# Last fourth-product rows at the end, fewer matmuls in the second half, sums by accumulating DMAs: one change to an FFT-convolution and MLP kernel

## The chip, the cores and the metric

The kernel runs on one core of one Trainium2 chip. The metric is the device time of one execution in microseconds (us); three runs of a kernel give its median. The engines are PE (matrix products into PSUM), ACT (activations, and nearly all copies out of PSUM), DVE (elementwise work), POOL (small work, and the issue of some DMAs) and SP (the issue of most DMAs).

## What is computed

The reference, cut to what matters (2048 rows, 640 columns, bf16 throughout):

```
x = A_q;  g = sigmoid((x * gate_w).sum(-1))
# a: long convolution
kv = (short 4-tap convolution of k along the rows) * v
y  = irfft(rfft(kv padded to 4096) * rfft(ssm_k padded to 4096))[:2048] + kv * ssm_D
a  = x * y
# b: two small MLPs
h  = gelu(layernorm(x) @ w1)                 # 640 -> 640
x1 = x + (h, four column groups shifted by 1, -1, 2, -2 rows) @ w2
b  = x1 + gelu(layernorm(x1) @ w3) @ w4      # 640 -> 1536 -> 640
out = g * a + (1 - g) * b
```

## The kernel before, in words

Everything lives in one SBUF tensor, `arena`. Row `1024 c + 8 p + rho` of an input lies on partition p, so the 2048 rows are 16 tiles (c = 0, 1; rho = 0 to 7) of 128 x 640. `X` holds x, later x1, later b, and in the end the output.

**The MLP side.** `ln1_rows` normalizes a pair of tiles on DVE (tag xn), transposes it on PE in ten pieces (xTp) and copies the result with one ACT operation of 1280 elements (xTe). Then come the first product (mm1, `gelu1`), the second (mm2, evicted to x1, with sums of squares on ACT), the second layernorm with transposes by DMA (xT, issued by SP), the third product (mm3: ten matmuls of 512 columns, `gelu3`) and the fourth (mm4: 24 matmuls of 320 columns for one tile). mm3 and mm4 run over four groups of rows, `sc` = 0 to 3, with six mm3 jobs and four mm4 jobs each. A job is a set of matmuls into one of four pairs of PSUM banks, with its evictions.

**The convolution side.** DVE makes kv from k and v (tags kv, kvb) in four blocks. The long convolution is a real transform of length 4096, split by hand: matmuls with cosine tables make parts of the transform (`forward`, fwdh for ssm_k and fwdk for kv), and DVE does the rest of it elementwise. It works on two halves of 320 columns (half 0, 1) and on two sets of 128 frequencies (kap = 0, 1). `unit(half, kap, ...)` is DVE's part: a `butterfly` of each signal (bh, bk), a `window` of kv, the complex product (`pointwise`, pw, pwz) and a `fold`. It is written in operations of 2560 and 1280 elements per partition. In each unit one addition of 2560 elements is done by a DMA that adds into its destination (`add_dma`, tag pwa, issued by POOL). For even r the transform of set 1 is got from the PSUM sums of set 0 with one more weight (`FM2`, two matmuls); for odd r it takes four matmuls of its own (`FM1`). `inverse(half, ...)` makes eight products, one for each rho, of eight matmuls each, evicts them with the gate g as scale (gy), multiplies them by q on DVE (fin), adds them to X, and stores. In half 0 that last sum is an accumulating DMA (fina); in half 1 it is DVE's, and the last four products are split into pieces of 320 (invl, gyl, finl).

**The order.** Nothing runs by loops at run time. The program collects nodes (one instruction or one matmul job each) with their dependences, and `schedule` puts them in one order with the help of a list of ranks and a forward model; each engine then executes its nodes in that order, waiting on semaphores. SP's and POOL's DMAs are nodes of their queues and stand in order as well: a waiting one holds those behind it.

The names and lines that the prediction uses: L663 is DVE's `tensor_tensor`, L694 every eviction by ACT, L1147 mm4, L1129 mm3, L1178 the transforms (`forward`), L1366 and L1341 the inverse products, L927 the transposes of the first layernorm, L702 `add_dma`, L868 a small POOL operation of the layernorms, L706 loads, L912 and L906 small layernorm operations on DVE.

Of the kernel before, what the change touches and what calls it, by code (L numbers as in the profile page):

```python
# [7 lines left out]
U16 = mybir.dt.uint16  # L8
# [4 lines left out]
PAIRS = 4  # L13
# [75 lines left out]
class Prog:  # L89
    LAT = {"pe": (0.0, 0.20), "act": (0.24, 0.16), "dve": (0.12, 0.12), "pool": (0.2, 0.2), "sp": (0.1, 0.1)}  # L90
    LOOK = 1.0

# [86 lines left out]
    PRIO = ()  # L179

    def schedule(self):
        for n in self.nodes:
            n.base = frozenset(n.deps)
        for j in self.jobs:
            own = set(j.nodes)
            j.ext = [d for v in j.nodes if not v.first for d in v.base if d not in own]
            if j.seeded:
                j.nodes[0].soft = [d for v in j.pes for d in v.base if d not in own]
        for n in self.nodes:
            for d in n.deps:  # L190
                d.users.append(n)
        for n in self.nodes:
            n.prio = self.PRIO[n.idx]
        self._forward()

    RATE = 390e3
    WINDOW = 3.4133
    PHASE = 2.4

    def _forward(self):  # L200
        nodes = self.nodes
        for n in nodes:
            n.deps = set(n.base)
            n.missing = len(n.deps)
            n.start = n.end = None
        for j in self.jobs:
            j.pair = None
            j.left = len(j.evicts) if j.evicts else 1
        free = {"pe": 1.0, "act": 0.7, "dve": 0.8, "pool": 1.1, "sp": 0.7}
        ready = {e: [] for e in ENGS}  # L210
        known_at = {}
        pair_free = [0.0] * PAIRS
        pair_job = [None] * PAIRS
        bits = [[False, False] for _ in range(PAIRS)]
        link = 0.0
        xlink = 0.0
        alink = 0.0
        slink = 0.0
        warm = False
        window = -1  # L220
        duty = carry = 0.0
        busy, lock = False, 0.0
        LAT = self.LAT

        def arrive(n):
            at = 0.0
            for d in n.deps:
                t = d.end + (LAT[d.eng][0 if d.eng == n.eng else 1] if d.kind == "c" else 0.05)
                if t > at:
                    at = t  # L230
            known_at[n] = at
            ready[n.eng].append(n)

        for n in nodes:
            if n.missing == 0:
                arrive(n)
        left = len(nodes)
        order = {e: [] for e in ENGS}
        allseq = []
        while left:  # L240
            best = None
            for e in ENGS:
                for n in ready[e]:
                    t = max(known_at[n], free[e])
                    if n.first:
                        j = n.job
                        tp = None
                        for i in range(PAIRS):
                            if pair_job[i] is not None and pair_job[i].left:
                                continue  # L250
                            if j.seeded and not (bits[i][0] and bits[i][1]):
                                continue
                            if tp is None or pair_free[i] < tp:
                                tp = pair_free[i]
                        if tp is None:
                            continue
                        t = max(t, tp)
                        ok = True
                        for d in j.ext:
                            if d.end is None:  # L260
                                ok = False
                                break
                            if not n.seed:
                                t = max(t, d.end - n.cost)
                        if ok and n.seed:
                            for d in n.soft:
                                if d.end is None:
                                    ok = False
                                    break
                                t = max(t, d.end - self.LOOK)  # L270
                        if not ok:
                            continue
                    key = (t, -n.prio, n.idx)
                    if best is None or key < best[0]:
                        best = (key, n)
            assert best is not None, "schedule is stuck"
            n = best[1]
            e = n.eng
            t = best[0][0]
            ready[e].remove(n)  # L280
            n.start = t
            cost = n.cost
            if n.array:
                w = int((t - self.PHASE) // self.WINDOW)
                while window < w:
                    warm = duty > (0.42 if warm else 0.75) * self.WINDOW
                    window += 1
                    duty, carry = carry, 0.0
                if not warm:
                    cost += n.array  # L290
                if n.tag != "shk":
                    inside = min(cost, self.PHASE + (w + 1) * self.WINDOW - t)
                    duty += inside
                    carry += cost - inside
            if n.kind == "c" and e == "pool":
                if busy and free["dve"] > t + 0.2:
                    cost *= 2.2
                lock = t + cost
            elif e == "dve":
                busy = n.cost > 0.3 and n.tag[:2] != "bn"  # L300
                if busy and lock > t + 0.1:
                    cost += 0.48
                    lock = 0.0
            free[e] = t + cost
            if n.kind == "xpose":
                free[e] = max(free[e], link - 1.5)
            if n.kind == "c":
                n.end = t + cost
            elif n.kind == "dma":
                link = max(link, xlink, t + 1.2) + n.bytes / self.RATE  # L310
                n.end = link + n.land
            elif n.kind == "acc":
                alink = link = max(alink, link, t + 1.2) + n.bytes / 220e3
                n.end = alink + 1.6
            elif n.kind == "side":
                slink = max(slink, t + 1.0) + 0.2
                n.end = slink + (6.5 if link > t else 2.8)
            else:
                xlink = max(xlink, t + 1.3, link) + n.bytes / 190e3
                n.end = xlink + 0.5  # L320
            j = n.job
            if n.first:
                pick = None
                for i in range(PAIRS):
                    if pair_job[i] is not None and pair_job[i].left:
                        continue
                    if j.seeded and not (bits[i][0] and bits[i][1]):
                        continue
                    if pick is None or pair_free[i] < pair_free[pick]:
                        pick = i  # L330
                j.pair = pick
                if pair_job[pick] is not None:
                    old = pair_job[pick]
                    n.deps.update(old.evicts if old.evicts else old.pes)
                pair_job[pick] = j
                for b in range(2):
                    if j.bits[b] is not None:
                        bits[pick][b] = j.bits[b]
            if j is not None and (n in j.evicts or not j.evicts):
                j.left -= 1  # L340
                if j.left == 0:
                    ends = [v.end for v in (j.evicts or j.pes)]
                    pair_free[j.pair] = max(ends) + 0.1
            n.seq = len(allseq)
            n.ordinal = len(order[e])
            order[e].append(n)
            allseq.append(n)
            left -= 1
            for u in n.users:
                u.missing -= 1  # L350
                if u.missing == 0:
                    arrive(u)
        self.order = order
        self.allseq = allseq
        self.span = max(n.end for n in nodes if n.tag[:4] != "fill")
        while order["pe"][-1].tag[:4] == "fill":
            order["pe"].pop()
# [37 lines left out]
    def emit(self, block):  # L395
# [11 lines left out]
        for n in self.nodes:  # L407
            if n.kind != "c":
                n.sem = nc.alloc_semaphore(f"d{n.idx}")
# [104 lines left out]

def _tables():

# [929 lines left out]
```

## Time and profile before

| what | value |
|---|---|
| three runs | 225.59, 225.94, 227.07 us, median 225.94 |
| profiled execution, first to last instruction | 223.5 us (of this execution no other time is listed; the median of the runs is 2.4 us longer than its span) |
| PE, DVE, ACT, POOL busy | 97%, 93%, 78%, 18% of the span |
| granted TensorE clock, mean | 0.998 |
| DMA traffic | 34.04 MB, mean 152 GB/s |

How to read it: "busy" is the union of an engine's instructions, so PE at 97% has hardly a gap. Rows of a view by form read: line, engine, operation, output and input shape, count, then busy time in us and mean time of one in ns, then the engine's idle time just ahead of them with who ended it. DMA rows give the count, the size and the median us from issue to landing.

### The profile page before, as it was taken

Reading aid. Unit: us, or ns where it says so; the run is one execution under the profiler, and the core shown is the slowest. Engines: PE = TensorE matmul, PEld = TensorE weight load, DVE = VectorE, ACT = ScalarE, POOL = GpSimd, SP = SyncE. Lnnn points to the kernel's source line nnn. Section 1 sums busy time; section 2 is a strip of 40 time slices with the busy share of each in tenths; the row PEclk is TensorE's granted clock in tenths of the full one; section 3 lists DMA queues with packets and bytes.
Section 4 is the critical chain, followed back from the end, with each engine's and each line's share of the span. In section 5 each row is a group of like instructions: output and inputs, shape, how many; then the busy total and the mean of one; then the engine's idle time right before and its main releaser. Section 6 shows DMA issues by size and latency. Waiting matters only on the chain.

```text
span 223.5 us, 3945 instructions
## 1 busy us (share of the span) xinstructions
PE 216.3 (97%) x1557; PEld 138.0 (62%) x1569; DVE 208.7 (93%) x267; ACT 174.6 (78%) x292; POOL 41.1 (18%) x48
## 2 busy tenths in 40 slices
PE   7999999999999999999999999999999999999993
PEld 7589655557676655457744455667745675577772
DVE  4999899999999899999899999799998999999976
ACT  3989999899999999999987488997145723572484
POOL 1335662403003120450200200000020002033020
PEclk9999999999999999999999999999999999999999
DMA  6999996589801968061654150003559000648667
GB/s 208 385 403 387 350 361 236 116 156 283 349 5 33 345 120 337 4 117 41 126 101 90 24 97 0 1 3 98 137 87 257 11 0 3 117 87 117 151 117 235
DMA packets 36713, 34.04 MB, mean 152 GB/s; under 512 B 17508, under 2 KB 31719, under 8 KB 36568
## 3 DMA queue, kind: packets, MB, share of 16 engines
q1 hardware_dynamic: 31560, 23.97, 35.8%
q0 software_dynamic: 4848, 9.50, 18.9%
q10 hardware_dynamic: 288, 0.33, 0.6%
q8 instruction: 12, 0.20, 0.4%
q14 instruction: 5, 0.04, 0.1%
HBM read 21.47 MB, written 3.93 MB: 114 GB/s over the span
## 4 chain that ended last, share of the span: by engine, by line
PE 76%; ACT 18%; DVE 2%; DMA 2%; issue 1%; SPq 0%; ACTq 0%
PE PS L1147 23%; PE PS L1129 23%; ACT arena L694 12%; PE PS L1178 9%; PE PS L967 8%; PE PS L1366 6%; ACT PS L1057 5%; PE PS L927 2%; ACT arena L680 2%; DVE arena L663 2%; DMA arena<-in_A_q_dram 2%; PE PS L823 1%; PE PS L769 1%; PE PS L758 1%; PE PS L780 0%
## 5 line engine op out<-in xcount | busy, mean ns | idle before, releaser
L663 DVE TENSOR_TENSOR arena<-arena 128x2560 bf16<-128x2560 bf16 (+5 forms) x175 | 186.1, 1116 | 7.0 <-ACT arena L694 3.5
L694 ACT ACTIVATE arena<-PS 128x640 bf16<-128x640 f32 (+8 forms) x142 | 104.2, 812 | 18.9 <-PE PS L1129 14.7
L1147 PE MATMUL PS<-arena 128*128 128x320 bf16 x384 | 53.3, 299 | 0.0
L1129 PE MATMUL PS<-arena 128*128 128x512 bf16 x232 | 52.2, 379 | 0.8 <-ACT arena L694 0.5
L1147 PEld LDWEIGHTS PS<-arena 128*128 128x128 bf16 x384 | 37.4, 98 | 15.0 <-issue 0.3
L694 ACT ACTIVATE arena<-PS,arena 128x320 bf16<-128x320 f32 (+1 forms) x47 | 27.7, 626 | 24.2 <-PE PS L1147 22.2
L1129 PEld LDWEIGHTS PS<-arena 128*128 128x128 bf16 x240 | 23.3, 98 | 27.4 <-issue 0.5
L1178 PE MATMUL PS<-arena 128*128 128x320 bf16 x224 | 34.4, 300 | 0.7 <-DVE arena L906 0.6
L1178 PEld LDWEIGHTS PS<-arena 128*128 128x128 bf16 x224 | 20.8, 98 | 12.8 <-ACT arena L694 2.8
L680 ACT ACTIVATE arena<-arena 128x640 bf16<-128x640 bf16 (+2 forms) x34 | 25.8, 787 | 0.8 <-DMA arena<-in_A_q_dram 0.4
L967 PE MATMUL PS<-arena 128*128 128x512 bf16 (+1 forms) x121 | 22.9, 335 | 0.2
L1075 PE MATMUL PS<-arena 128*128 128x320 bf16 x160 | 22.6, 299 | 0.0
L1057 ACT ACTIVATE PS<-arena 128x640 f32<-128x640 bf16 x32 | 22.3, 719 | 0.2
L868 POOL TENSOR_TENSOR arena<-arena 128x4 f32<-128x4 f32 (+1 forms) x9 | 14.0, 1553 | 30.7 <-DVE arena L668 30.4
L1075 PEld LDWEIGHTS PS<-arena 128*128 128x128 bf16 x160 | 15.4, 98 | 6.7 <-ACT PS L1057 0.6
L967 PEld LDWEIGHTS PS<-arena 128*128 128x128 bf16 x125 | 11.8, 98 | 8.2 <-ACT arena L694 0.5
L702 POOL DMA_DIRECT2D arena<-arena x4 | 4.8, 1202 | 57.6 <-DVE arena L663 57.6
L888 DVE BATCH_NORM_STATS2 arena<-arena 128x6 f32<-128x320 bf16 x28 | 12.4, 477 | 2.9 <-DMA arena<-in_A_q_dram 2.8
L1366 PE MATMUL PS<-arena 128*128 128x320 bf16 x96 | 14.3, 299 | 0.0
L1007 POOL DMA_DIRECT2D arena<-arena x18 | 9.7, 545 | 12.7 <-ACT arena L694 12.7
L1366 PEld LDWEIGHTS PS<-arena 128*128 128x128 bf16 x96 | 9.2, 98 | 4.3 <-issue 0.3
L1392 POOL DMA_DIRECT2D arena<-arena x4 | 5.1, 1276 | 35.7 <-ACT arena L694 25.9
(42 smaller groups left out, 81.5 us busy)
## 6 DMA issues: line engine op xcount, KB each, us to landing
arena<-in_B_w_dram POOLq DMA_DIRECT2D x4, 960.0 KB, 8.2
arena<-in_A_k_dram SPq DMA_DIRECT2D x4, 640.0 KB, 14.3
arena<-in_A_v_dram SPq DMA_DIRECT2D x4, 640.0 KB, 14.1
arena<-arena POOLq DMA_DIRECT2D x4, 640.0 KB, 6.1
arena<-in_A_q_dram SPq DMA_DIRECT2D x4, 640.0 KB, 7.4
out_dram<-arena SPq DMA_DIRECT2D x15, 160.0 KB, 2.0
arena<-in_A_q_dram SPq DMA_DIRECT2D x6, 320.0 KB, 5.5
arena<-in_A_ssm_k_dram SPq DMA_DIRECT2D x3, 512.0 KB, 11.5
```

The lines of the kernel that those rows point to most:

```text
L663: return dve(lambda e: e.tensor_tensor(o, a, b, op), [a, b], [o], c_tt(n), tag=tag, **kw)
L680: node = P.op("act", lambda e, ps: e.activation(o, i, func, **kw), r=r, w=[o], cost=c_act(n, naps, acc is not None, psum=False), tag=tag, ...
L694: node = P.op("act", lambda e, ps: e.activation(ov, inner(ps), func, **kw), r=r, w=[o], cost=c_act(n, len(r), acc is not None), job=job, t ...
L868: P.op("pool", lambda e, ps: e.tensor_tensor(r, v, hv, ALU.pow), r=[v, HALF], w=[r], cost=cost, tag="ln")
L888: dve(lambda e, o=o, x=x: e.bn_stats(o, x), [x], [o], 0.393, tag="bn", group=("bn", id(mv), rho, c))
L967: fns.append(lambda e, ps, b=b, c=c, lhsT=lhsT: e.matmul(bank(ps, b, 256 * n), lhsT, XT[:, c, r0:r0 + n, :], start=(c == 0), stop=(c == 4)))
L1057: P.seed(job, lambda e, ps: e.activation(two(ps, 320), x, ACTF.Copy), [X[:, c, rho, :]], c_act(640, psum=False), tag)
L1075: fns.append(lambda e, ps, hh=hh, ft=ft, lhsT=lhsT: e.matmul(bank(ps, hh, 320), lhsT, w2v[:, ft, 320 * hh:320 * hh + 320], start=False, st ...
L1129: fns.append(lambda e, ps, b=b, ft=ft, c=c, sc=sc: e.matmul(bank(ps, b, 512), w3h[ft // 6][:, c, 128 * (ft % 6):128 * (ft % 6) + 128], XT[ ...
L1147: fns.append(lambda e, ps, hh=hh, ft=ft, lhsT=lhsT: e.matmul(bank(ps, hh, 320), lhsT, w4h[ft // 6][:, ft % 6, 320 * hh:320 * hh + 320], st ...
L1178: fns.append(lambda e, ps, w=w, b=b, rhs=rhs, st=(first and n == 0), en=(n == len(ss) - 1): e.matmul(bank(ps, b, 320), w, rhs, start=st, s ...
L1366: fns.append(lambda e, ps, w=w, z=z, c=c, st=(n == 0), en=(n == len(terms) - 1): e.matmul(bank(ps, c, 320), w, z[:, c, :], start=st, stop=en))
```

## The change

1. The order is no longer computed by a forward model. A list of ranks (`RANK`, 981 numbers) gives the order of all nodes and a second one (`PAIR`) the PSUM pair of each job. DMA semaphores are shared where an earlier wait allows it.
2. mm4 of the last group (`sc` = 3) moves behind the inverse products in the program. Each of its four jobs is split: 12 matmuls of the first 320 columns, an eviction by ACT and an addition on DVE; 12 matmuls of the other 320, and one DVE operation that reads PSUM and adds. The added tensors are the finished g * q * y of both halves. In the new order of PE the first of these eight half jobs stands ahead of the first inverse product of half 1, the others alternate with these products, and two half jobs are last. So rows rho = 6, 7 are stored once, with 640 columns; the other rows are stored per half as before.
3. `R4M`: in half 1 the odd transforms of set 1 are also got from the sums of set 0 (two matmuls for four). The butterflies of that set are then "turned": four operations of 1280 become four of 640 and four of 1280.
4. `EVEN`: in half 1 the four inverse products with even r use two terms in place of four. Four DVE operations of 1280 (mir, mira) prepare them.
5. `BY_DMA`: in half 1 the first sum of each butterfly (4 of 2560), both inner sums of each product (8 of 1280) and two sums of each fold (4 of 1280) are accumulating DMAs; in half 0 those inner sums of the products that were DMAs already, now in pieces of 1280 (4). With fina there are 24 of them.
6. `unit` is rewritten as `units`, with `butterfly`, `product` (once for each half of the buffer) and `fold` in operations of mostly 1280 elements, which the order interleaves.
7. `LN1_DMA`: rows rho = 6, 7 of the first layernorm are transposed by four DMAs (xTd) from SP. In SP's new order they stand ahead of the last k load and of three of the eight w2 loads.
8. Scales 2 and sqrt 2 move into evictions, and the inverse table is divided by 2048.

The diff, cut to its core:

```
-FILL = 96
-PW1 = (0, 1, 2, 3)
-EVEN = ()
-LAST_SPLIT = 4
-FIN2 = {0: 4, 1: 0}
-FIN_DMA = (0,)
+FILL = 96
+FIN2 = (0,)
+EVEN = (1,)
+INV = {0: (0, 4, 2, 6, 1, 5, 3, 7), 1: (1, 5, 3, 7, 0, 4, 2, 6)}
+LN1_DMA = (6, 7)
+BY_DMA = {("pwa", 0, 0), ("pwa", 0, 1), ("pwa", 1, 0), ("pwa", 1, 1), ("fin", 0), ("bh", 1, 0), ("bk", 1, 0), ("bh", 1, 1), ("bk", 1, 1), ("fold", 1, 0), ("fold", 1, 1)}
+BY_DMA = BY_DMA | {("pwb", 1, 0), ("pwb", 1, 1)}
+R4M = {("h",1),("k",1)}
...
+    def schedule(self, rank, pairs):
+        for n in self.nodes:
+            n.prio = rank[n.idx]
+        self.allseq = sorted(self.nodes, key=lambda n: -n.prio)
+        self.order = {e: [n for n in self.allseq if n.eng == e] for e in ENGS}
...
+        if rho in LN1_DMA:
+            for c in range(2):
+                o = XT[:, :, rho, 128 * c:128 * c + 128]
+                P.dma("sp", lambda e, ps, o=o, b=bufs[c]: e.dma_start_transpose(o, b), ...
...
+    def mm4(sc, i):
+        parts = ((0, 1),) if sc < 3 else ((0,), (1,))
+        for hhs in parts:
...
+            elif hhs[0] == 0:
+                x, q = o[:, 0:320], Qh[0][:, c, rho, :]
+                evict(job, x, lambda ps: bank(ps, 0, 320), ACTF.Copy, 320, scale=omg, tag="Bl")
+                tt(x, x, q, ALU.add, 320, tag="finl")
+            else:
+                x, q = o[:, 320:640], Qh[1][:, c, rho, :]
+                P.op("dve", lambda e, ps, x=x, q=q, omg=omg: e.scalar_tensor_tensor(
+                    out=x, in0=bank(ps, 1, 320), scalar=omg, in1=q, op0=ALU.mult, op1=ALU.add),
...
-                if r % 2 == 0:
+                if r % 2 == 0 or (sig, half) in R4M:
...
+    def add_acc(o, i, n, tag):
+        return P.dma("pool", lambda e, ps: e.dma_start(o, i, accum_op=ALU.add, max_dma_last_dim=2560), ...
...
+    def butterfly(name, diff, other, turned, dma, tag):
+        lo, hi, D, T = hs(name + "a"), hs(name + "b"), hs(diff), hs(other)
+        tt(D, lo, hi, ALU.subtract, 2560, tag=tag + "d")
+        add(lo, hi, 2560, dma, tag + "a")
...
+    def product(H, K, temp, out_, da, db, tag):
+        tt(rb[0], kb[0], hb(1, 1), ALU.mult, 1280, tag=tag)
+        tt(tb[1], kb[1], hb(1, 0), ALU.mult, 1280, tag=tag)
+        add(T[:, 4:8], R[:, 0:4], 1280, da, tag + "a")
+        tt(rb[1], kb[0], hb(0, 1), ALU.mult, 1280, tag=tag)
+        tt(kb[1], kb[1], hb(0, 0), ALU.mult, 1280, tag=tag)
+        add(K[:, 4:8], R[:, 4:8], 1280, db, tag + "b")
+        tt(tb[0], kb[0], hb(1, 0), ALU.mult, 1280, tag=tag)
+        tt(kb[0], kb[0], hb(0, 0), ALU.mult, 1280, tag=tag)
+        tt(o[:, :, 0], k[:, :, 0], t[:, :, 1], ALU.subtract, 1280, tag=tag + "z")
+        tt(o[:, :, 1], k[:, :, 1], t[:, :, 0], ALU.add, 1280, tag=tag + "y")
...
+    def fold(T, S, A, B, dma, tag):
+        tt(E[:, 0:4], S[:, 0:4], S[:, 4:8], ALU.subtract, 1280, tag=tag + "d")
+        tt(E[:, 4:8], T[:, 0:4], T[:, 4:8], ALU.subtract, 1280, tag=tag + "d")
+        add(S[:, 0:4], S[:, 4:8], 1280, dma, tag + "a")
+        add(T[:, 0:4], T[:, 4:8], 1280, dma, tag + "a")
+        tt(Bx[:, 0:4:3], E2, E3, ALU.subtract, 1280, tag=tag + "t")
+        tt(Bx[:, 2:0:-1], E2, E3, ALU.add, 1280, tag=tag + "t")
+        tt(A[:, 0:4], S[:, 0:4], T[:, 0:4], ALU.add, 1280, tag=tag + "s")
+        tt(A[:, 4:8], S[:, 0:4], T[:, 0:4], ALU.subtract, 1280, tag=tag + "s")
...
+    def inverse(half, Y0, Y1, temp):
+        for a in range(2 * (half in EVEN)):
+            x, y = x4[:, a], (y4[:, a] if a == 0 else y4[:, a, ::-1])
+            tt(t4[:, a], x, y, ALU.subtract, 1280, tag=f"mir{a}")
+            add(x, y, 1280, ("mir", half) in BY_DMA, f"mira{a}")
...
+    Qh[1] = load_q(1, "k1")
+    inverse(1, Y[1][0], Y[1][1], "s3a")
+    for i in range(4):
+        mm4(3, i)
+    P.schedule(RANK, PAIR)
```

More of the change, by code (lines that the diff above doesn't have):

```diff
@@ L189, in schedule @@
         for n in self.nodes:
             for d in n.deps:
[L191 to L357, printed above, removed]
@@ L1310, in mirror @@
[L1310 to L1320 removed]
+        x4, y4, t4 = [v.rearrange("p (a i b) d -> p a i b d", a=2, i=2) for v in (Y0[0], Y1[0], hs(temp))]
@@ L1402, in inverse, with bydma, units @@
         P.stage = ""
+    def bydma(what, half, kap):
+        return (what, half, kap) in BY_DMA
+    Y = [[], []]
+    parts = {}
+    def units(half, plan):
+        for step in plan:
+            what, kap = step[0], step[1]
+            P.stage = 2 * half + kap
+            if what in ("bh", "bk"):
+                if what == "bk":
+                    window(step[2], kap)
+                parts[what] = butterfly(step[2], step[3], step[4], kap == 1 and (what[1], half) in R4M,
+                                        bydma(what, half, kap), what)
+            elif what == "pw":
+                parts["y"] = [product(parts["bh"][i], parts["bk"][i], step[2 + 2 * i], step[3 + 2 * i],
+                                      bydma("pwa", half, kap), bydma("pwb", half, kap), "pw" + "TS"[i]) for i in range(2)]
+            else:
+                Y[half].append(fold(*parts["y"], step[2], step[3], bydma("fold", half, kap), "fold"))
+        P.stage = ""
```

498 lines of the change are left out of this document (239 added, 259 removed), and 93 rows, old and new, of tables (PAIR, RANK).

## The prediction

> **What bounds the kernel now.** I read the page's busy times first, then the chain's last steps, then PE and DVE in single stretches. The columns of the chain are start, us, what; those of a timeline are start, us, engine, line, operation, count, and in brackets the idle time before it and who ended it.
>
> ```profile
> span 223.5 us, 3945 instructions
> PE 216.3 (97%) x1557; PEld 138.0 (62%) x1569; DVE 208.7 (93%) x267; ACT 174.6 (78%) x292; POOL 41.1 (18%) x48
> ...
> 152.54 9.78 PE PS L1147 x72
> ...
> 217.01 3.98 DVE arena L663 x15
> 220.99 0.02 issue
> 221.02 0.33 DVE arena L663
> ...
> 215.83 3.97 PE L1341 MATMUL PS<-arena 128*128 128x320 bf16 x28
> ```
>
> Two engines are full. PE is busy for 216.3 of 223.5 us, and at its own pace: 72 matmuls of 320 columns in 9.78 us, 0.136 us each. Its last matmuls end at 219.8 (215.83 + 3.97). DVE is busy for 208.7 us, and the chain ends in 15 short DVE operations without a gap: at 217.0 DVE still had 4 us of the last inverse products to finish. Behind its end at 221.35 come 2.15 us for the last store. So a gain needs less PE work, no more DVE work, and an end where neither queues behind the other.
>
> Next DVE by form from the first butterfly to the last fold (74.8 to 212.2), and single waits.
>
> ```profile
> L663 DVE TENSOR_TENSOR arena<-arena 128x2560 bf16<-128x2560 bf16 x58 | 83.9, 1488 | 3.2 <-ACT arena L694 1.6 <-DMA arena<-arena 1.0
> L663 DVE TENSOR_TENSOR arena<-arena 128x1280 bf16<-128x1280 bf16 x64 | 49.1, 821 | 0.5 <-ACT arena L694 0.2
> ...
> L906 DVE SCALAR_TENSOR_TENSOR arena<-arena 128x4 f32<-128x4 f32 x3 | 0.5, 159 | 0.7 <-ACT arena L680 0.7
> ...
> 27.78 0.18 DVE L663 TENSOR_TENSOR arena<-arena 128x16 f32<-128x16 f32 x1 [0.93 <-POOL arena L868]
> ...
> 69.58 3.08 DVE L663 TENSOR_TENSOR arena<-arena 128x2560 bf16<-128x2560 bf16 x2
> ...
> 72.81 5.31 PE L1178 MATMUL PS<-arena 128*128 128x320 bf16 x36 [0.56 <-DVE arena L906]
> ...
> 143.63 5.96 DVE L663 TENSOR_TENSOR arena<-arena 128x2560 bf16<-128x2560 bf16 x6 [1.65 <-ACT arena L694]
> ```
>
> In these 137.4 us DVE waits 3.2 + 0.5 + 0.7 = 4.4 and works 133.0. The two large forms and some 3.5 us of small ones add up to 136.5, since each form's busy time includes the overlap with its neighbours; I scale by 133.0/136.5 = 0.974. That gives 1.41 us for 2560 elements (83.9/58) and 0.747 for 1280 (49.1/64). The rows at 69.58 and 72.81 are one event: the last kv product ends at 72.66, and PE starts the transforms of kv right behind it.
>
> **The change part by part. PE.** In the second half the second frequency set drops two of four matmuls in each odd transform: 2 signals x 2 rows x 2 (real, imaginary) x 2 = 16. Four of its eight inverse products take 4 matmuls for 8: 16 more. 32 x 0.136 = 4.35 us, all in the stretch where PE is full. Rows 6 and 7 of the first layernorm lose 20 transposes on PE and two evictions on ACT:
>
> ```profile
> 31.59 1.12 PE PS L927 x20
> ...
> L694 ACT ACTIVATE arena<-PS 128x1280 bf16<-128x1280 bf16 x8 | 9.8, 1237 | 0.0
> ...
> arena<-in_A_q_dram SPq DMA_DIRECT2D x4, 640.0 KB, 7.4
> ...
> arena<-in_A_k_dram SPq DMA_DIRECT2D x4, 640.0 KB, 14.3
> ...
> arena<-arena SPq DMA_TRANSPOSE x16, 2.7
> ...
> 19.91 2.69 SPq L706 DMA_DIRECT2D arena<-in_A_k_dram  x3
> ...
> 22.60 1.44 DVE L663 TENSOR_TENSOR arena<-arena 128x2560 bf16<-128x2560 bf16 x1
> ```
>
> These 1.12 us of PE and 2.5 us of ACT I cost at nothing: they lie ahead of the transforms of kv, which wait for DVE's kv product anyhow. What hides them is DVE's kv work; without that cover they were a gain of 1.1 us. In their place SP issues four transposing DMAs, and the new order of SP puts them ahead of the third k load and three small loads, where before all k loads were issued by 22.6 (19.91 + 2.69). The last of the four waits for DVE's normalization of row 6, which in the new order stands behind one operation of 5120 elements (2.8 us), five of 2560 and four short ones: about 22.6 + 2.8 + 7.1 + 1.7 = 34.2. Two transposes at 1.3 us and one small load later SP issues the k load, at 37.3. DVE reads these rows one 5120 and six 2560 operations later, at 45.5. A 640 KB load took 7.4 us (q) to 14.3 us (k, behind a full queue): landing 44.7 to 51.6, a wait of 0 to 6.1 us. I take 0, since by 37 the queue ahead of it is nearly empty, and keep 6.1 for the range.
>
> **DVE.** Per unit of the first half 15 operations of 2560 and 14 of 1280 become 4 and 36: 2 x (22 x 0.747 - 11 x 1.41) = +1.9 us. In the second half four adds of 2560 and eight of 1280 go to accumulating DMAs, the second set's butterflies gain eight operations of 640, and four of 1280 prepare the shared inverse products: 28 of 2560 and 32 of 1280 become 4, 68 and 8 of 640. The forms of the end:
>
> ```profile
> L663 DVE TENSOR_TENSOR arena<-arena 128x320 bf16<-128x320 bf16 x15 | 3.9, 320 | 0.0
> L663 DVE TENSOR_TENSOR arena<-arena 128x640 bf16<-128x640 bf16 x8 | 3.8, 489 | 1.4 <-ACT arena L694 1.4
> L1351 DVE SCALAR_TENSOR_TENSOR arena<-PS,arena 128x320 bf16<-128x320 f32 x1 | 0.5, 544 | 0.0
> ```
>
> With 0.475 for 640: -24 x 1.41 + 36 x 0.747 + 8 x 0.475 = -3.1 us. The last products of the second half go from 8 of 640, 15 of 320 and one of 0.54 (8.2 us) to 14, 4 and 4 (9.9 us): +1.7. Together +0.5: DVE's work stays what it was. What moves is its place. The last fold need no longer be followed by inverse matmuls and then 4 us of DVE alone; the fourth product now gives PE work to the end.
>
> **The sum.** The wait of 0.93 goes, as another kv product now stands in it: kv ends at 72.66 - 0.93 = 71.7. From there to the last odd part of the last fold, after which PE can finish, the new order of DVE holds 12 operations of 2560, 136 of 1280, 8 of 640 and some 3.8 us of small ones: 16.9 + 101.6 + 3.7 + 3.8 = 126.0, so 197.7. PE then still has 32 + 16 matmuls of inverse products and 7 half jobs of 12 for the fourth product: 132 x 0.136 = 17.9, so 215.6. DVE's own rest beside it is smaller (5.2 + 9.9 = 15.1) and is hidden. PE's own sum agrees: 219.8 - 4.35 = 215.5. Behind PE stand 0.2 us to wake DVE, 0.54, and the store, 2.15: 218.5. Both engines arrive together, so each wait of DVE before 197.7 counts in full.
>
> Which waits? The 1.65 on ACT should go: in the two order tables, at 0.136 us a matmul of 320 columns, about 15 us less PE work (third and fourth products) stands ahead of the last of the second half's first-set transforms. The accumulating DMAs grow from 8 to 24, all through POOL's queue.
>
> ```profile
> arena<-arena POOLq DMA_DIRECT2D x4, 640.0 KB, 6.1
> ...
> arena<-arena POOLq DMA_DIRECT2D x4, 320.0 KB, 4.5
> ...
> L702 POOL DMA_DIRECT2D arena<-arena x4: 1177/1196/1238, 94.5 to 196.9; - x4
> ...
> DMA to landing us min/median/max: 5.6/6.1/7.0
> ...
> 122.04 10.88 DVE L663 TENSOR_TENSOR arena<-arena 128x1280 bf16<-128x1280 bf16 x8
> ...
> 126.09 1.22 POOL L702 DMA_DIRECT2D arena<-arena  x1 [14.23 <-DVE arena L663]
> ...
> 24.03 2.82 DVE L663 TENSOR_TENSOR arena<-arena 128x5120 bf16<-128x5120 bf16 x1
> 24.21 3.54 POOL L868 TENSOR_TENSOR arena<-arena 128x4 f32<-128x4 f32 x1 [2.96 <-DVE arena L668]
> ```
>
> In the new order DVE has 8 to 10 us of other work between the issue of a 640 KB add and its first reader, and 4.5 to 8 for the 320 KB adds of the products and of the first fold: enough at 4.5 us, not at 7.0. (The last fold's adds have only 3 us, but their readers lie behind 197.7.) At 7.0 six places would wait 0.4 to 2.3 us, 7.8 in all. I take 1.0, near 4.5, for the thinnest places: 219.5. The issues cost DVE nothing: POOL's issue at 126.09 lies inside a row of one 1280 and seven 2560 operations that took 10.88, against 10.6 by my prices.
>
> [...]
>
> **Rivals.** (1) Forecast, 0.60: span 219.5, alone 218 to 221. (2) No change, 0.21: DVE stays the clock and its old waits come back in new places, 4.4 us in place of 1.0, or the k load lands late by 4: 218.5 + 4.4 to 5 = 223 to 223.5. For it: DVE's work does not shrink. Against: its largest single wait had a cause that moves. (3) Slower, 0.10: the 320 KB adds land at 7.0 us and more, because several stand in one queue; 7.8 us at the six places: 226.3. It decides from a landing of about 6.9 us. Against: 4.5 in the trace, though with one add in flight at a time. (4) Slower, 0.03: POOL's issue holds DVE for its length, 16 x 1.2 = 19 us: 238. (5) Better, 0.06: the kv work ends earlier still and PE's 1.1 us counts too: 218.5 - 1.1 = 217.4.
>
> **How the numbers follow.** The median of the runs shown is 225.94, 2.4 above the profiled span; I add 2.4 to each span. Forecast 221.9; rivals 225.4 to 225.9, 228.7, 240, 219.8. A difference under 1% (223.7 to 228.2) cannot be told from none here. Faster: 0.60 + 0.06 = 0.66; within: 0.21; slower: 0.13. The range leaves out (3) and (4) above and part of (5) below: 218.8 to 226.8.
>
> **What would show it.** Right: PE busy near 212 with 32 matmuls fewer; the chain ends in matmuls of the fourth product, one DVE operation and a store, no DVE row of 4 us; DVE busy 207 to 210; DVE's waits on accumulating DMAs under 2 us in all. Wrong: DVE waits on the k load near 45 us; DVE rows waiting for DMA in the second half's products and folds, with landings over 6.9 us; PE idle for several us before the first half's inverse products, which need DVE's fold; DVE operations of 1280 elements above 0.82 us.

## The result, and the profile after

The changed kernel takes 224.88 us (median of 20 runs, 222.86 to 226.48) against 226.05 for the kernel before, a ratio of 0.995. Without its three slowest runs (226.27 and more, which count as slow) the ratio is 0.992 (95% interval 0.990 to 0.994). The forecast was 221.9, that is -1.8%; measured is -0.5 to -0.8%, which lies inside the 1% that the text had called no change. The profiled execution is the longest of the 20 (226.48 us, mean clock 0.985). Its page, and then the steps of its chain that end it (start, us, what):

```profile
span 224.4 us, 3910 instructions
...
PE 216.7 (97%) x1520; PEld 136.3 (61%) x1520; DVE 205.3 (91%) x307; ACT 171.3 (76%) x291; POOL 62.0 (28%) x64
...
PEclk9859999999999999999999999999999999999999
...
arena<-arena POOLq DMA_DIRECT2D x18, 320.0 KB, 4.6
...
arena<-arena POOLq DMA_DIRECT2D x4, 640.0 KB, 6.1
```

```profile
217.46 3.27 PE PS L1033 x24
220.74 0.02 issue
220.76 0.55 DVE arena L1046
```

The end has the form that was forecast: matmuls of the fourth product (L1033), one DVE operation, a store. The accumulating DMAs land as forecast, 4.6 and 6.1 us. But PE is busy for 216.7 us, not 212, and the clock row has an 8 and a 5 near its start. Three places differ from the forecast. The first is the granted clock, here by stretches of 5 us (PE busy and its instructions, PEld, DVE, ACT, POOL, clock, DMA share, GB/s), two rows of before, then three of after:

```profile
5.00:10.00 5.00, 4.44 (x58) 2.98 (x57) 4.40 (x15) 4.53 (x12) 0.92 (x2) 1.00 1.04 374
10.00:15.00 5.00, 5.00 (x45) 3.39 (x43) 4.50 (x17) 4.29 (x7) 2.85 (x4) 1.00 1.03 405
```

```profile
5.00:10.00 5.00, 4.35 (x48) 3.18 (x46) 4.31 (x16) 3.75 (x12) 0.71 (x1) 1.00 1.00 343
10.00:15.00 5.00, 5.00 (x26) 2.69 (x25) 4.97 (x19) 3.98 (x5) 2.42 (x3) 0.50 1.05 393
15.00:20.00 5.00, 5.00 (x34) 3.49 (x33) 4.94 (x18) 2.97 (x6) 0.00 (x0) 0.82 1.03 410
```

From 10 to 15 us PE gets half its clock and runs 26 matmuls where before ran 45, although it looks fully busy. Of the 20 runs of the changed kernel, 11 have a mean clock of 0.992 or less (median 225.56 us), nine 0.997 or more (224.18). Of the 48 runs of before made beside the experiments, eight are below 0.997. So a lower mean clock is not new with the change, but more frequent.

The second place is POOL's order. The timeline of after, DVE, then POOL, then PE (in brackets the wait and who ended it):

```profile
22.05 0.80 DVE L554 TENSOR_SCALAR arena<-arena 128x640 bf16<-128x640 bf16 x2 [1.86 <-POOL arena L756]
...
20.26 0.61 POOL L901 DMA_DIRECT2D arena<-arena  x1 [5.62 <-ACT arena L580]
20.90 1.04 POOL L756 TENSOR_TENSOR arena<-arena 128x4 f32<-128x4 f32 x1
...
32.99 4.28 POOL L901 DMA_DIRECT2D arena<-arena  x8 [3.68 <-ACT arena L580]
37.29 3.11 POOL L721 TENSOR_TENSOR arena<-arena 1x320 bf16<-1x320 bf16 x1
...
40.46 3.16 PE L1091 MATMUL PS<-arena 128*128 128x320 bf16 x22 [1.29 <-POOL arena L721]
```

POOL waits 5.62 us for a gelu of ACT ahead of a small DMA (a "tail" of the MLP's shift), and the layernorm operation that DVE needs (L756) stands behind it: DVE waits 1.86. Then eight tails stand ahead of the operation that puts ssm_D into the taps (L721), and PE's transforms wait 1.29 for that. In the kernel before as many tails stand ahead of ssm_D's operation (L833), but their data come earlier:

```profile
19.18 1.03 POOL L868 TENSOR_TENSOR arena<-arena 128x4 f32<-128x4 f32 x1
20.16 1.08 POOL L1007 DMA_DIRECT2D arena<-arena  x2
...
27.71 2.18 POOL L1007 DMA_DIRECT2D arena<-arena  x4
29.91 0.91 POOL L833 TENSOR_TENSOR arena<-arena 1x320 bf16<-1x320 bf16 x1
```

The third is SP's queue at the end:

```profile
215.88 5.50 SPq L1273 DMA_DIRECT2D out_dram<-arena  x9
221.43 0.99 SPq L1052 DMA_DIRECT2D out_dram<-arena  x2
```

DVE's last operation ends at 220.76 + 0.55 = 221.31. SP is then still issuing the other stores at some 0.5 us each (L1273's twelve take 0.498 us in the median); the last of the two final stores goes out at about 221.97, and from DVE's end to the end of the span it takes 3.1 us, where before it took 2.15.

In between the sum comes out. DVE's waits in after, over the whole span (who waited for whom: us in total, times, longest), and then two rows of its timeline that date the stages:

```profile
DVE arena L549 <- ACT arena L580: 4.6, 7, 1.2
...
DVE arena L554 <- POOL arena L756: 1.9, 1, 1.9
DVE arena L794 <- ACT arena L580: 1.5, 1, 1.5
...
DVE arena L549 <- DMA arena<-arena: 0.7, 1, 0.7
```

```profile
72.73 3.02 DVE L549 TENSOR_TENSOR arena<-arena 128x2560 bf16<-128x2560 bf16 x3
...
193.27 8.57 DVE L549 TENSOR_TENSOR arena<-arena 128x1280 bf16<-128x1280 bf16 x11
```

The accumulating DMAs cost DVE 0.7 us of waiting in all. The row at 72.73 begins with the last kv product, which so ends at 74.2 (forecast 71.7); the row at 193.27 ends with the last odd part of the last fold, at 201.84. That stretch took 127.6 us; the forecast had 126.0 + 1.0 of waits. DVE is busy for 124.4 us of it and waits 3.2, for ACT (1.2), POOL (0.9), DMAs (0.7) and in small gaps.

### The profile page after: what moved, and what is told of

Its sections match the earlier page's. It is cut to its first block, busy times and chain, and to the rows that moved or that the text cites. A ratio compares the mean times of both kernels' runs of the same rounds, so it can differ in the third digit from the quotient of the medians.

```text
span 224.4 us, 3910 instructions
## 1 busy us (share of the span) xinstructions
PE 216.7 (97%) x1520; PEld 136.3 (61%) x1520; DVE 205.3 (91%) x307; ACT 171.3 (76%) x291; POOL 62.0 (28%) x64
## 4 chain that ended last, share of the span: by engine, by line
PE 66%; ACT 25%; POOL 3%; DMA 2%; DVE 1%; SPq 1%; issue 0%
PE PS L1033 23%; PE PS L1062 16%; ACT arena L580 16%; PE PS L861 8%; PE PS L1234 7%; PE PS L1091 6%; ACT arena L566 5%; ACT PS L953 4%; DMA arena<-in_A_q_dram 2%; POOL arena L901 2%; PE PS L821 2%; PE PS L711 1%; POOL arena L721 1%; PE PS L656 1%; PE PS L667 1%; SPq L592 1%
## 5 line engine op out<-in xcount | busy, mean ns | idle before, releaser
L549 DVE TENSOR_TENSOR arena<-arena 128x1280 bf16<-128x1280 bf16 (+5 forms) x212 | 182.3, 923 | 6.8 <-ACT arena L580 4.6
L580 ACT ACTIVATE arena<-PS 128x640 bf16<-128x640 f32 (+7 forms) x140 | 104.8, 814 | 22.9 <-PE PS L1062 8.0
L1033 PE MATMUL PS<-arena 128*128 128x320 bf16 x384 | 54.4, 299 | 0.5 <-ACT arena L580 0.5
L1062 PE MATMUL PS<-arena 128*128 128x512 bf16 x240 | 54.3, 379 | 0.0
L1033 PEld LDWEIGHTS PS<-arena 128*128 128x128 bf16 x384 | 37.5, 98 | 15.5 <-issue 0.8
L1121 POOL DMA_DIRECT2D arena<-arena x24 | 24.0, 1107 | 71.1 <-DVE arena L549 66.5
L580 ACT ACTIVATE arena<-PS,arena 128x320 bf16<-128x320 f32 (+1 forms) x48 | 26.5, 603 | 21.2 <-PE PS L1033 15.2
L1091 PE MATMUL PS<-arena 128*128 128x320 bf16 x208 | 33.3, 300 | 1.7 <-POOL arena L721 1.3
L566 ACT ACTIVATE arena<-arena 128x640 bf16<-128x640 bf16 (+2 forms) x34 | 28.5, 865 | 2.0 <-DMA arena<-in_A_q_dram 1.8
L756 POOL TENSOR_TENSOR arena<-arena 128x4 f32<-128x4 f32 (+1 forms) x9 | 18.7, 2077 | 27.4 <-DVE arena L554 23.9
L861 PE MATMUL PS<-arena 128*128 128x512 bf16 (+1 forms) x125 | 24.4, 353 | 0.0
L971 PE MATMUL PS<-arena 128*128 128x320 bf16 x160 | 22.9, 299 | 0.0
L1234 PE MATMUL PS<-arena 128*128 128x320 bf16 x112 | 17.0, 299 | 0.0
L901 POOL DMA_DIRECT2D arena<-arena x18 | 9.7, 544 | 16.2 <-ACT arena L580 16.2
L645 PE MATMUL PS<-arena 128*128 128x128 bf16 x81 | 10.5, 277 | 1.2 <-DVE arena L602 1.2
```

The costliest lines, as they stand in the source:

```text
L549: return dve(lambda e: e.tensor_tensor(o, a, b, op), [a, b], [o], c_tt(n), tag=tag, **kw)
L566: node = P.op("act", lambda e, ps: e.activation(o, i, func, **kw), r=r, w=[o], cost=c_act(n, naps, acc is not None, psum=False), tag=tag, ...
L580: node = P.op("act", lambda e, ps: e.activation(ov, inner(ps), func, **kw), r=r, w=[o], cost=c_act(n, len(r), acc is not None), job=job, t ...
L756: P.op("pool", lambda e, ps: e.tensor_tensor(r, v, hv, ALU.pow), r=[v, HALF], w=[r], cost=cost, tag="ln")
L861: fns.append(lambda e, ps, b=b, c=c, lhsT=lhsT: e.matmul(bank(ps, b, 256 * n), lhsT, XT[:, c, r0:r0 + n, :], start=(c == 0), stop=(c == 4)))
L971: fns.append(lambda e, ps, hh=hh, ft=ft, lhsT=lhsT: e.matmul(bank(ps, hh, 320), lhsT, w2v[:, ft, 320 * hh:320 * hh + 320], start=False, st ...
```

## The experiments

**e1: the changed kernel once more**, for a second profile.

> The changed kernel once more, for a second profile. The first profile of it has a granted clock of 0.83 in its first 20 us, and there PE falls 3 us behind its own work (PE's start against the sum of the work ahead of it: 4.6 us at 9.6 us, 7.6 us at 19). Theory A (the time was lost in the first 75 us by the order of the queues): also at full clock DVE waits some 1.9 us at 20 us for POOL's layernorm operation behind the first tail DMA, the last kv product ends after 73 us (forecast 71.7), and PE waits over 1 us at 40 us for POOL's ssm_D operation. Theory B (it was the clock of that one profile): at full clock these waits go, kv ends near 71.7, and the span is near the forecast of 219.5. Theory C (PE's own work was saved less than forecast): kv ends near 71.7, PE has no waits, and the span is still 222.

225.19 us in one run, span 223.1, clock 0.991:

```profile
10.00:15.00 5.00, 5.00 (x29) 3.00 (x30) 5.00 (x18) 4.00 (x5) 2.42 (x3) 0.66 1.05 397
```

The dip costs half as much: 0.34 x 5 = 1.7 us of full clock, against 3.4 in after. DVE's wait for POOL at 20 us shrinks to 0.71, PE's for ssm_D stays (1.27), and kv ends at 72.7. An undisturbed profile came only with e5 (clock 0.999): there DVE's wait at 20 us is gone, PE's is 1.89, DVE still waits 1.52 us for ACT at 68.9, and kv ends at 72.1, for a span of 221.7. So B holds for DVE's early wait and A for PE's. C, PE without waits, does not; but in e5 too the part behind kv is 1.8 us longer than forecast (149.6 against 147.8).

**e2: two nodes of POOL moved ahead.**

```
+RANK[252] = 798.5    # POOL's layernorm operation of rows 4, 5: ahead of the first tail
+RANK[182] = 746.5    # the first ssm_D operation: ahead of the other tails
```

> The changed kernel with two nodes of POOL moved ahead: the layernorm operation of rows 4 and 5 in front of the first tail DMA, and the first ssm_D operation in front of the seven tail DMAs. Theory A: DVE's wait of 1.9 us at 20 us and PE's wait of 1.3 us at 40 us go, both engines start the long stretch 1 to 2 us earlier, and the time falls by 1 to 2 us against the changed kernel (to about 0.985 of the kernel before). Theory B and C: no difference from the changed kernel (0.992).

224.14 us, ratio 0.989 (0.981 to 0.997). Four runs only: 222.17 at a clock of 1.0, and 224.09 to 225.46 at 0.981 to 0.992. In the profile, which has the same early dip as e1 (0.67), both waits are gone, kv ends at 71.8 and the span is 222.0, 1.1 less. From kv on, DVE's rows are those of e1, 0.9 us earlier: what is gained in the head is kept to the end. In the median it is clouded by the clock.

**e3, e8: a third of a row group's fourth product left out**, early and late.

```
-                for ft in range(12):
+                for ft in range(12 if sc else 8):        # e3;  e8: 8 if sc == 1 else 12
```

> The changed kernel with a third of the matmuls of the fourth product of the first row group left out: 32 of 320 columns, 4.35 us of PE at 102 to 115 us, where PE has no gap. If PE alone sets the end: 4.3 us less than the changed kernel (0.973 of before). If DVE alone sets it: no difference. Both engines within 1 us of each other, as the first profile has it (the last fold ends at 201.85, the inverse product that needs it starts at 202.63): 0.8 to 1.2 us less (0.988).

> The changed kernel with a third of the matmuls of the fourth product of the second row group left out: 32 of 320 columns, 4.35 us of PE at 150 to 166 us. In the earlier such run (first row group, 102 to 115 us) nothing was gained: PE's next transform at 115.33 started at the same time, behind ACT. If PE sets the pace from 115 us on: 4.3 us less (0.973). If PE and DVE arrive within 1 us of each other at the last fold, as in the profile: 0.8 to 1 us less, and PE waits for the last fold (0.988). If ACT still sets it: nothing.

Neither gained: e3 225.59 us (0.998, 0.994 to 1.001), e8 226.35 (0.999, 0.997 to 1.002), both above the changed kernel's median, at lower clocks. First two stretches of e1 (the fourth sum is ACT's); then PE at the place where the removed work ends, in e1 and in e3:

```profile
90.00:105.00 15.00, 14.46 (x83) 7.98 (x83) 14.85 (x28) 15.00 (x28) 6.01 (x5) 1.00 0.82 235
105.00:115.00 10.00, 10.00 (x76) 7.14 (x73) 10.00 (x15) 10.00 (x17) 2.57 (x1) 1.00 0.44 84
```

```profile
115.10 0.23 PE L645 MATMUL PS<-arena 128*128 128x128 bf16 x1
115.16 1.79 PE L1091 MATMUL PS<-arena 128*128 128x320 bf16 x12
```

```profile
115.09 0.23 PE L645 MATMUL PS<-arena 128*128 128x128 bf16 x1 [2.02 <-ACT arena L580]
115.16 1.79 PE L1091 MATMUL PS<-arena 128*128 128x320 bf16 x12
```

The 4.35 us turned into waits on ACT (4.2 us in this stretch, the last of them the 2.02 shown; 0.5 in e1), and the transform starts at 115.16 in both: up to there ACT, which has no gap (15.00 of 15, 10.00 of 10), is as full as PE. In e8, the wait at the last fold, and the stretch behind it:

```profile
199.62 2.03 PE L1234 MATMUL PS<-arena 128*128 128x320 bf16 x8 [2.98 <-DVE arena L549]
```

```profile
200.00:205.00 5.00, 5.00 (x27) 2.99 (x26) 3.53 (x6) 1.48 (x3) 4.00 (x4) 0.66 1.01 150
```

PE now waits 2.98 us for DVE's fold, gains nothing, and is then granted 0.66: 27 matmuls in 5 us where the undisturbed number (e7) is 39. So some 12 matmuls, 1.6 us, were lost behind a wait of 3 us; that the wait lowered the clock is not shown. All ten runs of e8 have a clock of 0.992 or less, and its profile has no early dip. Eight of the ten of e3 are as low, and its profile has the early dip.

**e4: four DVE additions of the first half's folds cut to 16 elements** (2.7 us of DVE).

```
-        add(S[:, 0:4], S[:, 4:8], 1280, dma, tag + "a")      # and the same for T; only where not by DMA
+        tt(v[:, 0, 0:16], v[:, 0, 0:16], v[:, 4, 0:16], ALU.add, 16, tag=tag + "a")
```

> The changed kernel with the four DVE additions of 1280 elements in the folds of the first half cut to 16 elements: 2.7 us of DVE less. If DVE alone sets the end: 2.7 us less than the changed kernel (0.980 of before). If PE alone sets it, or both arrive together: no difference (0.992).

224.21 us, 0.990 (0.985 to 0.995); at 0.998 and more 222.89 to 224.29, as the changed kernel there. DVE gives most of it back in a wait of 2.41 us at 139 us on an eviction by ACT (0.50 there in e1): from 130 to 160 us it is busy for 27.52 us, in e1 for 29.43. PE alone, ACT's stretch and DVE alone: none is the limit by itself.

**e5, e6, e7: the fillers (matmuls whose results nobody reads), the first half's six stores issued by POOL, and all three repairs.**

```
+for n, (node, job) in enumerate(((136, 94), (109, 67), ...)):     # e5, e7: 14 spare fillers, 8 and 6
+    RANK[node] = (886.9 if n < 8 else 870.9) - 0.01 * n
+    PAIR[job] = 1 + n % 2 if n < 8 else n % 2
...
-                P.dma("sp", lambda e, ps, src=src, dst=dst: e.dma_start(dst, src), ...
+                P.dma("sp" if half else "pool", lambda e, ps, src=src, dst=dst: e.dma_start(dst, src), ...   # e6, e7
```

> The changed kernel with 14 of its spare filler matmuls (128 columns, results unused), which stood behind the end and were dropped, put into PE's two waits ahead of the first transposes (8 at about 6.5 us, 6 at about 8.5 us). In 11 of the 20 runs of the changed kernel the mean granted clock was 0.992 or less, and all four profiles of it and its variants have 0.50 to 0.67 granted from 10 to 15 us; its runs at 0.997 and more took 224.1 us in the median, those below 225.5. Theory D (too little PE work from 6 to 10 us, 3.6 to 4.4 us busy of 5 in the profiles, lets the clock be halved just behind it): with the fillers the granted clock is 0.997 or more in nearly all runs, and the median is 223.9 to 224.2 (0.990 to 0.992 of before, against 224.9 for the changed kernel). Theory E (the dip has nothing to do with PE's waits): dips in half of the runs as before, median 224.9.

> The changed kernel with the six stores of the first half issued by POOL, which is idle at the end, instead of SP. In the profile SP issues nine stores back to back to 0.5 us after DVE's last operation, and the last store is issued 0.9 us after its data are ready (220.66 against 219.80). Theory F (SP's queue of stores is late at the end): 0.8 us less, 0.9885 of before. If these stores are hidden: no difference (0.992).

> The fillers, POOL's two moved nodes and POOL's stores together. If the time was lost at three separate places (1.2 us for POOL's order, 0.8 us for SP's stores, some 0.8 us on average for the clock): 222.1 us, 0.982 of before, which is the forecast of 221.9. If the long stretch behind absorbs the gain of the head: 223.5 and more.

e5: 224.50 us, 0.992 (0.989 to 0.995): three runs at 0.998 and more took 223.57 to 223.78, three still had 0.991 to 0.992 and took 225.21 to 225.31, so theory D did not hold for fillers alone. e6: 224.57, 0.992 (0.988 to 0.995): 223.29 and 223.43 at a clock of 1.0, 225.1 in the middle of the others. Each alone hardly shows in the median. **e7: 221.66 us, 0.980 (0.978 to 0.983), all five runs at 1.0, a span of 219.5** — faster than both kernels, and the forecast's own span. Rows of its profile: the page's span, the stretch from 5 to 15 us, two stage rows of DVE and SP's last stores from the timeline, and the end of the chain:

```profile
span 219.5 us, 3940 instructions
```

```profile
5.00:10.00 5.00, 5.00 (x63) 3.70 (x61) 4.81 (x19) 4.38 (x12) 0.72 (x1) 1.00 1.01 376
10.00:15.00 5.00, 4.88 (x40) 3.06 (x40) 5.00 (x18) 4.99 (x7) 2.42 (x3) 1.00 1.05 395
```

```profile
68.72 3.02 DVE L556 TENSOR_TENSOR arena<-arena 128x2560 bf16<-128x2560 bf16 x3
...
193.31 4.01 DVE L556 TENSOR_TENSOR arena<-arena 128x1280 bf16<-128x1280 bf16 x5
...
216.43 1.17 SPq L1059 DMA_DIRECT2D out_dram<-arena  x2
```

```profile
213.38 3.27 PE PS L1040 x24
216.65 0.03 issue
216.68 0.55 DVE arena L1053
```

kv ends at 70.2, the last odd fold at 197.32, PE at 216.65.

**e9, e10, e11, e12: what a microsecond of PE and of DVE is worth in e7.** e9 takes back the shared inverse products; e10 issues the second set's odd transforms twice; e11 leaves out e8's matmuls and cuts four DVE products of the second half to 16 elements; e12 puts the sums of the second half's folds back on DVE.

```
-EVEN = (1,)                                          # e9, with the four ranks of mir and mira
+            if half and r % 2 and not first:         # e10
+                fns = fns + fns
+        if db:                                       # e11, besides e8's edit
+            tt(K[:, 0, 0:16], K[:, 0, 0:16], H[:, 0, 0:16], ALU.mult, 16, tag=tag)
-BY_DMA = {..., ("fold", 1, 0), ("fold", 1, 1)}       # e12
```

> The combined kernel (fillers, POOL's two nodes, POOL's stores; 0.980 of before) with the four shared inverse products of the second half back at eight matmuls each, and the four DVE operations that prepare them left out: 16 matmuls more, 2.2 us, all of them behind the last fold, where PE has no gap. If the saving was real at its place: 2.0 to 2.4 us more, 0.990. If the end is set by something else (stores, DVE): 0.980 to 0.983.

> The combined kernel with the two matmuls of each odd transform of the second set in the second half issued twice (its sums are then not the transform's): 16 matmuls more, 2.2 us of PE, at 120 to 165 us; DVE's work is unchanged. If PE has no slack from 113 us on: 2.0 to 2.4 us more, 0.990. If PE has slack there behind DVE: 0 to 1 us more, 0.980 to 0.985.

> The combined kernel with 32 matmuls of the fourth product of the second row group left out (4.35 us of PE at 150 to 166 us) and four DVE products of 1280 elements of the second half cut to 16 elements (2.7 us of DVE). Each alone brought nothing (DVE's in the first half). If PE and DVE are tied to each other at the last fold: now some 2.5 us less, 0.969. If a third thing (ACT, DMAs, the order) holds both: 0.978 to 0.980.

> The combined kernel with the four sums of the second half's folds (1280 elements each) on DVE again in place of accumulating DMAs: 4 x 0.735 = 2.9 us of DVE more; the two of the first set lie ahead of the last odd fold, those of the second set too in DVE's order. If DVE has no slack: 1.5 to 2.9 us more, 0.987 to 0.993. If DVE has slack behind PE: under 0.5 us more, 0.980 to 0.982.

| run | edit | us | against e7's 221.66 | ratio to before (interval) |
|---|---|---|---|---|
| e9 | PE +2.2 behind the last fold, four DVE operations there left out | 223.67 | +2.0 | 0.989 (0.985 to 0.992) |
| e10 | PE +2.2 at 120 to 165 us | 222.77 (one of four runs 225.94, at 0.992) | +1.1 | 0.990 (0.981 to 0.998) |
| e11 | PE -4.35 and DVE -2.7 ahead of it | 218.49 | -3.2 | 0.966 (0.962 to 0.971) |
| e12 | DVE +2.9 | 223.19 | +1.5 | 0.986 (0.983 to 0.990) |

Behind the last fold a microsecond of PE counts nearly in full (2.0 of 2.2). Ahead of it PE and DVE look tied: more work on either costs about half its length, less on one (e8, e4) brought nothing, less on both 3.2 us. The cuts on one engine were made in the changed kernel without the repairs, e4's in the first half and e11's in the second; neither was tried alone in e7, so the tie is argued in part.

**e13, e14: e7 without the stores, e7 without the fillers.**

> The combined kernel with the six stores back on SP: fillers and POOL's two moved nodes alone. If the late stores are a cause of their own: the last store is issued some 0.7 to 0.9 us after DVE's last operation, and the time is 0.7 to 0.9 us more than the combined kernel's 221.66 (0.984), at a clock of 1.0 in nearly all runs. If they are hidden: 0.980.

> The combined kernel without the fillers: POOL's two moved nodes and POOL's stores. If PE's waits between 6 and 10 us bring the clock dip: about half of the runs have a mean granted clock of 0.992 or less and take 1 to 1.5 us more than the others, 0.5 us of waits stay in the others too, and the median is 222 to 223 (0.983 to 0.987). If the dip came from the wait at 40 us for POOL (gone here): all runs at 1.0 and 0.980.

e13: 222.00 us, 0.981 (0.978 to 0.984), six runs at 0.997 to 1.0. The last store goes out 0.31 us after DVE's end, and the stores are worth 0.3 us, not 0.8: with the head repaired, the queue is less late. e14: 222.39, 0.982 (0.979 to 0.985): two runs at 1.0 took 221.35 and 221.50, as e7; four at 0.992 took 222.38 to 222.54. One dip costs 1.0 us there.

## Why the prediction was right or wrong

**Right by two misses: the long stretch.** From kv to the last odd fold DVE took 127.6 us in after and 127.1 in e7 (forecast 127.0). But it was busy for only 124.4 us of it in both, where the prices taken from before gave 126.0, and it waited 3.2 and 2.7 us, where I took 1.0. The page's 205.3 us for DVE lie below the 207 to 210 that were to show the forecast right.

**Right: the DMAs, the k load.** The DMAs land at 4.6 and 6.1 us and cost DVE 0.7 us of waits. DVE waited nothing for the k load, though its issue comes late:

```profile
33.87 5.61 SPq L818 DMA_TRANSPOSE arena<-arena  x4
...
40.15 0.42 SPq L592 DMA_DIRECT2D arena<-in_A_k_dram  x1
```

The two POOL rivals fell: the adds land at 4.6, not 7.0, and 24 issues of 24.0 us in all do not hold DVE, whose operations of 1280 elements are no longer than before:

```profile
L549 DVE TENSOR_TENSOR arena<-arena 128x1280 bf16<-128x1280 bf16 x144 | 108.8, 817 | 3.2 <-issue 1.2 <-ACT arena L580 0.8 <-DMA arena<-arena 0.7
```

The row is e1's, with a mean of 817 ns; in before it was 821 ns.

**Wrong: the first 72 us, "kv ends at 72.66 - 0.93 = 71.7".** This step took over the head of before and subtracted one wait. I had followed SP's queue past the new transposes, but not POOL's and PE's: the new ranks put eight tail DMAs ahead of ssm_D's operation, a tail that waits for ACT ahead of a layernorm operation, and fewer fillers between PE's early waits. In after kv ends at 74.2, the clock's part in it included; in e5, at a clock of 0.999, at 72.1. With POOL's two nodes moved (e13, 222.00) the kernel is 1.6 us faster than without at the same clock (e5 at 0.998 and more, 223.60), and kv then ends at 70.2 to 70.3. So that 71.7 lies within 0.4 of e5 is luck: the new order saves 1.5 us more in the head than I gave it, and POOL's order, which I did not follow, takes 1.8 back.

The rest is lost behind kv. The terms of the sum, in us:

| term | forecast | after (clock 0.985) | e5 (0.999) | e7 (1.0) |
|---|---|---|---|---|
| kv ends at | 71.7 | 74.2 | 72.1 | 70.2 |
| from there to the last odd fold, with waits | 127.0 | 127.6 | 127.9 | 127.1 |
| until PE starts the product that reads it | 0 | 0.8 | 0.6 | 1.2 |
| PE from there to its end | 17.9 | 18.1 | 18.1 | 18.1 |
| to the end of DVE's last operation | 0.7 | 0.6 | 0.6 | 0.6 |
| the store | 2.15 | 3.1 | 2.4 | 2.3 |
| span | 219.5 | 224.4 | 221.7 | 219.5 |

The rows behind the third line, in after and in e7 (the fold ends at 201.84 and 197.32), and two of e5, for kv and for the end:

```profile
202.63 1.25 PE L1234 MATMUL PS<-arena 128*128 128x320 bf16 x8
```

```profile
198.55 1.25 PE L1241 MATMUL PS<-arena 128*128 128x320 bf16 x8
```

```profile
70.57 3.02 DVE L554 TENSOR_TENSOR arena<-arena 128x2560 bf16<-128x2560 bf16 x3
```

```profile
215.39 3.27 PE PS L1038 x24
```

At an undisturbed clock (e5) the step "both engines arrive together" is wrong as well: DVE's stretch is 0.9 longer and PE reaches the fold's reader 0.6 after the fold. The 0.2 us to wake DVE stand in no row; its last operation starts 0.02 us behind PE's end in after and 0.03 in e7.

**Missing: the clock.** The sum used 0.136 us for a matmul everywhere. In 11 of 20 runs of after the mean clock is 0.992 or less, and the profiles with such a mean have a stretch of 5 us at 0.50 (after, e6) or 0.66 to 0.67 (e1 to e4, e8); that is 1.4 us between the medians of the two groups, and 1.0 in e14. With one repair of PE's waits alone dips remained: fillers alone three of six runs (e5), POOL's order alone three of four and four of six (e2, e14). With both, none of the 11 runs of e7 and e13, and one of the 16 of e9 to e12. Where the dips of e5 lay was not seen, since its one profile has none; PE's wait of 1.89 us for ssm_D is a place to suspect. What starts a dip stays open.

**Mis-sized: the store, "2.15", and the "2.4 above the profiled span".** The change leaves nine stores for SP in the last 6 us ahead of the final two, 0.5 us each: 3.1 us from DVE's end in after, 2.4 in e5. Stores on POOL bring 0.3 us beside the other repairs (e13), and 0.8 by the two undisturbed runs of e6 without them. The 2.4 set the median of the runs against the span of one of them. Where a run lists both, the time is about 2.1 us above the span (224.38 and 222.2 in after, 221.66 and 219.5 in e7), so the forecast's span stands for some 221.6 us.

Together, at an undisturbed clock: 224.18 for the changed kernel, 223.60 with the fillers, 222.00 with POOL's order too, 221.66 with the stores too, for a forecast of 221.9. POOL's order is the largest step; with it alone, e2's one run at a clock of 1.0 took 222.17. The clock lifts the changed kernel's median by another 0.7, to 224.88. That the fillers bring 0.6 beyond the clock is not sure: e14's two undisturbed runs are as fast as e7's.

**Right for a wrong reason: "32 x 0.136 = 4.35 us, all in the stretch where PE is full".** The text said that two engines are full. There are three: ACT holds PE until 115 us (e3), and from there PE and DVE seem to hold each other (e8, e10 to e12). PE, without dips and without the fillers (e14), is busy for 213.3 us, 3.0 less than before, where 4.35 was counted. The 16 inverse matmuls, behind the last fold, are worth the 2.0 of e9; the 16 forward ones, by e10, 1.1 of 2.2. And the sum came out of e7 by two misses: its fold is ready at 197.3 (forecast 198.7 with the waits), but PE reaches the product that needs it only 1.2 us later, and the slack of DVE is what e12 shows too (1.5 us for 2.9). PE's own sum, "219.8 - 4.35 = 215.5", which seemed to agree, is 1.1 us under e7's 216.65; the agreement of the two sums proved nothing.

The rival of no change had the right mechanism in kind, waits that come back in new places. On DVE's long stretch, where it looked, they are 3.2 us (it had 4.4), hidden in the sum by operations that took less than priced. At the k load there is none. The others were in the first 40 us and in the last 6, where it did not look.

## What to carry to other kernels

A change that hands out a whole new order moves every queue: check the head and the tail of each engine's order, POOL's and SP's too, for an instruction that others need behind one that waits (here POOL's 5.62 us), before pricing the middle. When several engines are tied, a cut on one shows as nothing (here e8 and e4); cut two at once to see the tie (e11, 3.2 us), and look for time where all wait together. A sum that comes out right can hold two misses: compare it with the trace term by term. Look at the granted clock behind a wait of PE as well: in e8 it was 0.66 in the 5 us behind a wait of 2.98 us, and some 1.6 us of matmuls were lost there.

## What the runs showed of the hardware

The granted clock was halved without PE being idle for long: in after PE was busy for 4.35 of the 5 us ahead of the drop, with a single wait of 0.65 us. In half microseconds the clock there is 0.50 to 0.51 from 10.0 to 16.5 us, 0.67 to 17.0 and 1.00 from then on. The busy time ahead does not decide it: with 4.72 us (e4) a drop came (0.66 from 10 to 15 us), with 4.34 (e14) and 4.45 (e8) none did (1.00). The lost share is 0.50 x 5 + 0.18 x 5 = 3.4 us of full clock in after, and 0.34 x 5 = 1.7 in e1 and in e8; the late drop in e8 stood behind a wait of 2.98 us. What starts a drop is not shown.

POOL's small arithmetic was of uneven length: the same ssm_D operation took 3.11 us in after, 1.29 in e7 and 0.91 in before, each time beside other operations of DVE. That these are the cause is not shown.
